# An attention kernel fused with a feed-forward layer: the order of the first steps' state, masks and weight casts, and of the last group's products

## The chip, the cores and the metric

The kernel runs on one core of a Trainium2 chip. The metric is the device time of one launch in microseconds (us); a smaller time is better. The median of three runs before the change is 206.12 us (206.1 to 206.34).

A core has five engines with an instruction queue each: TensorE (PE, matmuls, with PEld for its weight loads), VectorE (DVE), ScalarE (ACT), GpSimd (POOL) and SyncE (SP), which here only issues transfers. The engines run side by side, each in the order of its own queue, and wait for one another through semaphores. Matmul results go to PSUM; all other data of the core is in SBUF.

## The reference

Decayed linear attention in blocks of 64 tokens, then a feed-forward layer on its output. Inputs are float32; `q`, `k`, `v` have 4 batches, 8 heads, 768 tokens and 64 features.

```python
for b in range(nb):
    intra = einsum('bhic,bhjc->bhij', qb, kb) * Dmask      # Dmask = lam ** (i - j), lower triangle
    intra = einsum('bhij,bhjd->bhid', intra, vb)
    inter = einsum('bhid,bhde->bhie', qb * lam_pow, kv_state)
    out[:, :, sl] = intra + inter
    kv_state = lam_block * kv_state + einsum('bhsd,bhse->bhde', kb * rev_pow, vb)
x = attn_out.transpose(0, 2, 1, 3).reshape(3072, 512)
h = x @ w_in                      # 512 x 2048
out = gelu_tanh(h) @ w_out        # 2048 x 512
```

## The kernel before

**Attention steps.** The attention is cut into 24 steps. A step `s` is 256 tokens of one batch (a superblock, `sbg = s // 2`) and four of the eight heads (`half = s % 2`). Inside, the 256 tokens are two chunks `c` of 128. For each step:

- `prep_qk` and `prep_v` scale q and v by the decay and convert q, k and v to 16 bits (DVE, ACT, POOL); `stage_t` transposes q and k on PE into `Tps` and copies them to `qkT` (L245 to L251: which engine copies depends on the step).
- `scores` makes k times q in the PSUM tile `Sps`; `causal` (L280, DVE) multiplies it by the mask into `PT`.
- `products(n, s)` does two things on PE. For step `n` it makes the new part of the state, K, in columns 256 to 383 of the two PSUM tiles `OK` (L306). For step `s` it makes the output in columns 0 to 255: values times `PT` (L320), plus state `u` times q (L329). It takes two new PSUM tiles unless it is given `banks`.
- `update(s, c, parts)` carries the state on: part "t" (L366, DVE) reads K from `OK`, part "u" (L373, POOL) makes the 16-bit `u` that L329 reads.
- `x_out` (L343, ACT) copies the output of a step to `xT`, the transposed input of the feed-forward layer.

**Feed-forward groups.** The tokens are done in seven groups of 256 or 512 (L380). Group 0 is superblocks 0 and 1, thus steps 0 to 3. Its rows of `h` come from `mm1_part` (rows f = 0 to 7) and `mm1` (8 to 15): four matmuls over the 128-row pieces c of `x`, where pieces 0 and 1 are heads of the even steps and 2 and 3 those of the odd steps. A stage of `mm1_part` names the pieces, the token blocks (b0, b1 or both) and if it is the last, after which the GELU follows on ACT. Weights arrive as float32 and are cast: `cast_win` (L105 on ACT, L107 on DVE) for `w_in`, others for `w_out`.

From group 2 on the second product is done with seven half-sized products instead of eight (a Strassen-like scheme): `product(m, p)` for m in 3, 4, 5, 2, 1, 7, 6 and a pair p of 128-row tiles. Products 4 and 3 lie in PSUM tile A, 5 and 2 in B, 1 in C, 7 and 6 in D; for the last pair of all, 6 has a tile E. After product 2, ACT copies B (L477, L478) and DVE makes all four quarters of `o` from A and B (L481, L482); after product 1 DVE adds C to the two diagonal quarters (L490), after 7 and 6 it adds D (L502), in the last pair one quarter each (L497). Then the rows are stored.

**Order.** Everything is recorded in program order per engine (`pin`). Feed-forward work stands as small pieces in the list `filler`, and `fill(n)` puts the next n pieces at that place. The order of the first steps is written out by hand (L600 to L652). The last group's order is the product list built at L546 to L551.

PSUM tiles other than `Sps` share six buffers (`ps_M`), so a new tile waits until an old one is free.

Of the kernel before, what the change touches and what calls it, by code (L numbers as in the profile page):

```python
# [15 lines left out]
def kernel(  # L16
# [217 lines left out]
    def stage_t(s):  # L234
        if s >= FIRST_DMA_T:
            return
        tq, tk = a16[s][:2]
        Tps = ps_M.tile([P, 2, 2, 2, P], FP16, tag="M", name="Tps")
        for i, t in enumerate((tq, tk)):
            for hp in range(2):  # L240
                for j in range(2):
                    pin(nc.tensor.transpose(Tps[:, i, j, hp, :], t[:, j, 2 * hp : 2 * hp + 2, :],  # L242
                                            ident[:]))
        o = qkp.tile([P, 2, 2, 2, P], FP16, tag="qkT", name=f"qkT_{s}")
        if s == 2:  # L245
            pin(nc.scalar.activation(out=o[:, 0], in_=Tps[:, 0], func=AF.Copy))
            pin(nc.vector.tensor_copy(out=o[:, 1], in_=Tps[:, 1]))
        elif s in (1, 3, 5, 6):
            pin(nc.scalar.activation(out=o[:], in_=Tps[:], func=AF.Copy))
        else:  # L250
            pin(nc.vector.tensor_copy(out=o[:], in_=Tps[:]))  # L251
        qkT[s] = o
# [80 lines left out]
            x_out(s, OK)  # L333
        return OK, opened

    def x_out(s, OK):
        sbg, half = divmod(s, 2)
        g, i = group_of[sbg]
        if g not in xT:
            xT[g] = xtp.tile([P, 2, len(groups[g]), 2, SB], FP16, tag="xT", name=f"xT_{g}")  # L340
        dst = xT[g][:, half, i]
        for c in range(2):
            pin(nc.scalar.activation(  # L343
                out=dst[:, :, c * P : (c + 1) * P].rearrange("p hp (t j) -> p hp j t", j=2),
                in_=OK[c][:, 0:256].rearrange("p (hp j t) -> p hp j t", hp=2, j=2),
                func=AF.Copy))

    us = {}

# [34 lines left out]
    def queue_group(g):  # L384
# [60 lines left out]
                i = slice(i0, i1)  # L445
                pin(nc.vector.tensor_tensor(gsum[m][:, i, :], block(T0, F0, i), block(T1, F1, i), op))  # L446

        of_pair = {}
        PLACE = {4: ("A", 0), 3: ("A", 1), 5: ("B", 0), 2: ("B", 1), 1: ("C", 0), 7: ("D", 0),
                 6: ("D", 1)}  # L450

        def product(m, p):

            banks = of_pair.setdefault(p, {})
            name, half = PLACE[m]
            final = g == len(groups) - 1 and p == HN // P - 1
            if final and m == 6:
                name = "E"
            if m in (3, 5, 1, 7) or name == "E":
                banks[name] = ps_M.tile([P, 2, HE], FP32, tag="M", name=f"M{name}")  # L460
            dst = banks[name][:, half]
            t = slice(p * P, p * P + P)
            for i in range(HF):
                lhsT = block(*G_PLAIN[m], i)[:, t] if m in G_PLAIN else gsum[m][:, i, t]
                if m in W_PLAIN:
                    F, E = W_PLAIN[m]
                    rhs = w_out16[:, F * HF + i, E * HE : E * HE + HE]
                else:
                    rhs = w_sum16[:, w_slot[m], i, :]
                pin(nc.tensor.matmul(dst, lhsT, rhs, start=(i == 0), stop=(i == HF - 1),  # L470
                                     skip_group_check=True))
            tt = nc.vector.tensor_tensor
            if m == 2:
                o = banks["o"] = otp.tile([P, 2, 2, HE], FP32, tag="o32", name="o32")
                A, B = banks["A"], banks["B"]
                m525 = mtp.tile([P, 3, HE], FP32, tag="m525", name="m525")
                pin(nc.scalar.activation(out=m525[:, 0:2], in_=B[:], func=AF.Copy))  # L477
                pin(nc.scalar.activation(out=m525[:, 2], in_=B[:, 0], func=AF.Copy))  # L478
                flat = o[:].rearrange("p e t d -> p (e t) d")
                banks["diag"] = flat[:, 0:4:3]  # L480
                pin(tt(banks["diag"], A[:], m525[:, 0:2], ALU.subtract))  # L481
                pin(tt(flat[:, 1:3], A[:], m525[:, 1:3], ALU.add))  # L482
                if final:
                    for T, queue in ((1, nc.sync), (0, nc.scalar)):
                        row = row0 + T * HN + p * P
                        E = slice((1 - T) * HE, (1 - T) * HE + HE)
                        pin(queue.dma_start(out=out[row : row + P, E], in_=o[:, 1 - T, T, :]))
            elif m == 1:
                d = banks["diag"]
                pin(tt(d, banks["C"][:, 0].unsqueeze(1).to_broadcast([P, 2, HE]), d, ALU.add))  # L490
            elif final and m in (7, 6):

                o, T = banks["o"], (0 if m == 7 else 1)
                row = row0 + T * HN + p * P
                rows = out[row : row + P, :].rearrange("q (e d) -> q e d", e=2)
                d = o[:, T, T, :]
                pin(tt(d, banks[name][:, half], d, ALU.add))  # L497
                queue = nc.scalar if m == 7 else nc.sync
                pin(queue.dma_start(out=rows[:, T], in_=d))
            elif m == 6:  # L500
                d = banks["diag"]
                pin(tt(d, banks["D"][:], d, ALU.add))  # L502
                for T in range(2):
                    row = row0 + T * HN + p * P
                    pin(nc.sync.dma_start(out=out[row : row + P, :].rearrange("q (e d) -> q e d", e=2),
                                          in_=banks["o"][:, :, T, :]))
# [2 lines left out]

        def mm1_part(f, cs, blocks, last):  # L510

            if cs[0] == 0:
                first[f] = ps_M.tile([P, N], FP32, tag="M", name="Hps")
            for c in cs:
                pin(nc.tensor.matmul(by_block(first[f][:])[:, blocks],  # L515
                                     w_in16[:, c, f * P : (f + 1) * P], x(c)[:, blocks],
                                     start=(c == 0), stop=last and c == NC - 1,
                                     skip_group_check=True))
            if last:
                pin(nc.scalar.activation(out=gT[:, f % HF, f // HF, :], in_=first.pop(f)[:],  # L520
                                         func=AF.Gelu_apprx_tanh))

        if g == 0:
            both, b0, b1 = slice(0, 2), slice(0, 1), slice(1, 2)
            for fs, stages in ((range(4), (((0, 1), both, False), ((2, 3), b0, False),
                                           ((2, 3), b1, True))),
                               (range(4, 8), (((0, 1), both, False), ((2, 3), both, True)))):
                for stage in stages:
                    for f in fs:
                        filler.append(lambda f=f, stage=stage: mm1_part(f, *stage))  # L530
            for f in range(8, NF):
                filler.append(lambda f=f: mm1([f]))
            order = [(tau, part) for part in (0, 2, 1, 3) for tau in range(3)]
            order += [(3, part) for part in (0, 2, 1, 3)]
            for tau, part in order:
                filler.append(lambda tau=tau, part=part: mm2(tau, part))
            return
# [3 lines left out]
        if g == 1:  # L541
# [1 line left out]
                for part in (0, 2, 1, 3):  # L543
                    filler.append(lambda tau=tau, part=part: mm2(tau, part))
            return
        ms = ((3, 4, 5, 2), (1, 7, 6))  # L546
        order = [(m, p) for p in range(HN // P) for m in ms[0] + ms[1]]
        if g == len(groups) - 1:
            order = [(m, p) for part in ms for p in range(HN // P) for m in part]
        for m, p in order:  # L550
            filler.append(lambda m=m, p=p: product(m, p))  # L551

        def behind(k, i0, i1):

# [24 lines left out]
    def fill(n):  # L579
        for _ in range(min(n, len(filler))):  # L580
            filler.pop(0)()
# [36 lines left out]
    stage_t(2)  # L618
    prep_qk(3)
    update(1, 0)  # L620
    idle(3)
    scores(2)
    products(2, None)
    causal(2)
    prep_v(3)
    update(2, 0)
    update(1, 1)
    update(2, 1, "t")
    idle(2)
    stage_t(3)  # L630
    OK1 = products(None, 1, evacuate=False)[0]
    OK2 = products(None, 2, evacuate=False)[0]
    x_out(2, OK2)
    x_out(1, OK1)
    scores(3)
    banks = products(3, None)
    update(3, 0)
    c01, c23 = slice(0, 2), slice(2, 4)
    cast_win(0, 0, 256, 128, c01)
    cast_win(0, 256, 512, 256, c01, on_act=True)  # L640
    causal(3)
    queue_group(0)
    fill(4)
    products(None, 3, banks)
    cast_win(0, 0, 512, 256, c23)
    fill(8)
    cast_win(1, 0, 512, 256, c01)
    update(3, 1, "t")
    cast_win(1, 0, 512, 256, c23)
    fill(8)  # L650
    update(2, 1, "u")
# [83 lines left out]
```

## Time and profile before

The profiled execution took 206.1 us; its span, from the first to the last instruction, is 204.3 us.

| engine | busy us | share of the span | instructions |
|---|---|---|---|
| PE | 196.8 | 96% | 2321 |
| DVE | 144.8 | 71% | 271 |
| ACT | 107.7 | 53% | 204 |
| POOL | 70.1 | 34% | 80 |

The first 13.4 us hold the warm-up of PE (matmuls on ones), the first loads and steps 0 and 1. Transfers run at 381 GB/s from 13.4 to 20.7 us: inputs and weights come in one after the other on SP's queue. A profile row gives line, engine, operation, output and input tiles, count, then busy time and the mean of one; a timeline row begins with start and duration in us, and ends with the engine's idle time before it and what released it. Busy time of PE is that of pipelined matmuls, whose ends are modelled.

### The profile page before, as it was taken

How to read it: one execution, taken by the hardware profiler on the slowest of the kernel's cores; microseconds unless marked ns; L12 is line 12 of the kernel's file. 1: busy time of each engine (PE TensorE's matmuls, PEld its weight loads, DVE VectorE, ACT ScalarE, POOL GpSimd, SP SyncE). 2: the span in 40 equal slices, each digit the busy share in tenths (PEclk: the TensorE clock that was granted, in tenths of full speed). 3: DMA queues.
4: the chain of work that ended last, by engine and by line, in shares of the span. 5: the costliest groups of instructions: out<-in, count | busy, mean ns of one | idle time of the engine just before them, and what ended most of it. 6: DMA issues, size and time to landing. Idle time of an engine off the chain costs nothing.

```text
span 204.3 us, 5584 instructions
## 1 busy us (share of the span) xinstructions
PE 196.8 (96%) x2321; PEld 127.6 (62%) x2321; DVE 144.8 (71%) x271; ACT 107.7 (53%) x204; POOL 70.1 (34%) x80
## 2 busy tenths in 40 slices
PE   7888999999999999999999999999999999999992
PEld 2454644456875788654688654788554788545881
DVE  4887627867599999929997828996739673136552
ACT  2364678475683573477722477641576331577110
POOL 5595123646487750436134404314412100000000
PEclk9999999999999999999999999999999999999999
DMA  4999999999999999996449993647330003300014
GB/s 132 299 321 385 387 388 379 285 291 315 297 262 228 296 241 173 235 285 176 91 128 266 181 279 94 152 107 156 75 85 0 0 3 103 107 0 0 3 51 156
DMA packets 64074, 37.86 MB, mean 185 GB/s; under 512 B 17712, under 2 KB 59184, under 8 KB 64048
## 3 DMA queue, kind: packets, MB, share of 16 engines
q1 hardware_dynamic: 63760, 37.24, 68.1%
q8 instruction: 18, 0.29, 0.6%
q10 hardware_dynamic: 288, 0.26, 0.4%
q14 instruction: 8, 0.07, 0.1%
HBM read 27.27 MB, written 6.29 MB: 164 GB/s over the span
## 4 chain that ended last, share of the span: by engine, by line
PE 89%; DMA 3%; SPq 2%; ACT 1%; DVE 1%; issue 1%
PE Hps L401 37%; PE O2ps L416 10%; PE MB L470 8%; PE MA L470 7%; PE MD L470 7%; PE Sps L271 4%; PE MC L470 4%; PE Hps L515 4%; PE OK L329 3%; PE OK L320 3%; DMA k<-in_k_dram 3%; SPq L68 2%; PE OK L306 1%; PE Tps L242 1%; DVE t L366 1%
## 5 line engine op out<-in xcount | busy, mean ns | idle before, releaser
L401 PE MATMUL Hps<-xT,w_in 128*128 128x512 f16 (+1 forms) x416 | 79.1, 346 | 0.0
L405 ACT ACTIVATE gT<-Hps 128x512 f16<-128x512 f32 x88 | 52.1, 598 | 21.9 <-PE Hps L401 21.1
L401 PEld LDWEIGHTS <-w_in 128*128 128x128 f16 x416 | 40.2, 98 | 33.5
L373 POOL TENSOR_TENSOR u<-t,lumask 128x256 f16<-128x256 f32 x40 | 31.4, 792 | 80.6 <-DVE t L366 58.4
L446 DVE TENSOR_TENSOR gs<-gT 128x512 f16<-128x512 f16 (+1 forms) x70 | 36.6, 586 | 10.8 <-ACT gT L405 10.6
L280 DVE TENSOR_TENSOR PT<-Sps,mask 128x1024 f16<-128x1024 f32 x24 | 29.2, 1216 | 17.1 <-PE Sps L271 17.1
L470 PEld LDWEIGHTS <-gs 128*128 128x128 f16 x360 | 34.9, 98 | 4.0
L211 POOL TENSOR_TENSOR v<-v,dv 128x512 f16<-128x512 f32 x24 | 29.2, 1220 | 4.9 <-DMA v<-in_v_dram 4.8
L343 ACT ACTIVATE xT<-OK 128x256 f16<-128x256 f32 x48 | 18.2, 454 | 20.0 <-PE OK L329 14.3
L416 PE MATMUL O2ps<-w_out,gT 128*128 128x512 f16 x96 | 21.9, 379 | 0.0
L226 ACT ACTIVATE qk<-k 128x512 f16<-128x512 f32 x24 | 15.0, 626 | 9.3 <-DMA k<-in_k_dram 9.3
L221 DVE TENSOR_TENSOR qk<-q,dq 128x512 f16<-128x512 f32 x23 | 19.3, 841 | 0.0
L477 ACT ACTIVATE m<-MB 128x512 f32<-128x512 f32 x9 | 5.4, 597 | 25.4 <-PE MB L470 25.4
L470 PE MATMUL MA<-w_sum,gT 128*128 128x256 f16 x144 | 17.5, 273 | 0.1
L470 PE MATMUL MD<-w_sum,gs 128*128 128x256 f16 x136 | 17.5, 273 | 0.0
L470 PE MATMUL MB<-w_out,gs 128*128 128x256 f16 x144 | 17.2, 273 | 0.0
L366 DVE SCALAR_TENSOR_TENSOR t<-t,lamu,OK 128x64 f32<-128x64 f32 x64 | 14.5, 273 | 2.3 <-PE OK L306 1.1
L470 PEld LDWEIGHTS <-gT 128*128 128x128 f16 x144 | 14.0, 98 | 2.8 <-ACT gT L405 0.3
L416 PEld LDWEIGHTS <-gT 128*128 128x128 f16 x96 | 9.2, 98 | 9.9
L481 DVE TENSOR_TENSOR o<-MA,m 128x512 f32<-128x512 f32 x9 | 6.2, 688 | 12.3 <-ACT m L477 12.3
L271 PEld LDWEIGHTS <-qkT 64*64 64x64 f16 x384 | 6.2, 106 | 8.6 <-issue 4.2
L123 DVE TENSOR_TENSOR w_sum<-wo,wo 128x1024 f16<-128x1024 f32 x6 | 7.9, 1362 | 4.2 <-DMA wo<-in_moe_w_out_dram 4.2
(55 smaller groups left out, 168.8 us busy)
## 6 DMA issues: line engine op xcount, KB each, us to landing
q<-in_q_dram SPq DMA_DIRECT2D x24, 256.0 KB, 4.5
k<-in_k_dram SPq DMA_DIRECT2D x24, 256.0 KB, 4.9
v<-in_v_dram SPq DMA_DIRECT2D x24, 256.0 KB, 4.9
out_dram<-o SPq DMA_DIRECT2D x22, 256.0 KB, 4.1
wo<-in_moe_w_out_dram SPq DMA_DIRECT2D x4, 1024.0 KB, 9.2
wi<-in_moe_w_in_dram SPq DMA_DIRECT2D x4, 512.0 KB, 8.0
wi<-in_moe_w_in_dram SPq DMA_DIRECT2D x2, 1024.0 KB, 12.5
out_dram<-o SPq DMA_DIRECT2D x2, 128.0 KB, 1.9
```

The costliest lines, as they stand in the source:

```text
L211: pin(nc.gpsimd.tensor_tensor(wide(tv[:]), ld32[s][2][:], decay(dv, s), ALU.mult))
L221: pin(q_eng.tensor_tensor(wide(tq), q32[:], decay(dq, s), ALU.mult))
L226: pin(nc.scalar.activation(out=wide(tk), in_=k32[:], func=AF.Copy))
L280: pin(nc.vector.tensor_tensor(t[:].rearrange("p a b c d -> p (a b) (c d)"), Ss.pop(n)[:].rearrange("p a b c d -> p (a b) (c d)"), mask[:]. ...
L343: pin(nc.scalar.activation(out=dst[:, :, c * P : (c + 1) * P].rearrange("p hp (t j) -> p hp j t", j=2), in_=OK[c][:, 0:256].rearrange("p ( ...
L366: pin(nc.vector.scalar_tensor_tensor(t[:, hp, :], state[half][:, hp, :], lamu[:, 2 * half + hp : 2 * half + hp + 1], K[:, hp, :], ALU.mult ...
L373: pin(nc.gpsimd.tensor_tensor(u[:], state[half][:].unsqueeze(2).to_broadcast([P, 2, 2, D]), lumask[:, 2 * half : 2 * half + 2, :].unsqueez ...
L401: pin(nc.tensor.matmul(by_block(Hps[:, i, :]), w_in16[:, c, f * P : (f + 1) * P], x(c), start=(c == 0), stop=(c == NC - 1)))
L405: pin(nc.scalar.activation(out=dst, in_=Hps[:], func=AF.Gelu_apprx_tanh))
L416: pin(nc.tensor.matmul(O2[tau][0][:], gT[:, f % HF, f // HF, tau * P : (tau + 1) * P], w_out16[:, f, :], start=(n == 0), stop=(n == NF - 1)))
L446: pin(nc.vector.tensor_tensor(gsum[m][:, i, :], block(T0, F0, i), block(T1, F1, i), op))
L470: pin(nc.tensor.matmul(dst, lhsT, rhs, start=(i == 0), stop=(i == HF - 1), skip_group_check=True))
```

## The change

Five edits, in the order of the diff:

- The copy of `qkT` of step 3 is split: half on ACT, half on DVE, as that of step 2 was.
- `x_out` can put the second chunk on another engine. Step 3 uses it, with DVE.
- In the last group the product order is now pair by pair, all seven products of pair 0, then all of pair 1. Before, products 3, 4, 5, 2 of both pairs came first. The two stores of off-diagonal quarters right after product 2 are gone: with product 7 the lower one goes out on SP, and the upper rows in one store of 256 KB on ACT.
- The first rows f = 0 to 3 of group 0 do pieces 0 and 1 by token blocks as well: 16 matmuls of 256 columns instead of 8 of 512.
- The hand-written order of steps 2 and 3: the states of steps 1 and 2 ahead of step 2's mask; step 2's output into the tiles that hold its own K; steps 1 and 2 evacuated in that order; the second state of step 2 after its evacuation; the casts of `w_in` ahead of step 3's state and mask; part of the casts on ACT; step 3's output after ten filler pieces instead of four.

```diff
-        if s == 2:
+        if s in (2, 3):
             pin(nc.scalar.activation(out=o[:, 0], in_=Tps[:, 0], func=AF.Copy))
             pin(nc.vector.tensor_copy(out=o[:, 1], in_=Tps[:, 1]))
-        elif s in (1, 3, 5, 6):
+        elif s in (1, 5, 6):
...
-    def x_out(s, OK):
+    def x_out(s, OK, second=None):
...
         for c in range(2):
-            pin(nc.scalar.activation(
-                out=dst[:, :, c * P : (c + 1) * P].rearrange("p hp (t j) -> p hp j t", j=2),
-                in_=OK[c][:, 0:256].rearrange("p (hp j t) -> p hp j t", hp=2, j=2),
-                func=AF.Copy))
+            d = dst[:, :, c * P : (c + 1) * P].rearrange("p hp (t j) -> p hp j t", j=2)
+            o = OK[c][:, 0:256].rearrange("p (hp j t) -> p hp j t", hp=2, j=2)
+            if c == 1 and second is not None:
+                pin(second.tensor_copy(out=d, in_=o))
+            else:
+                pin(nc.scalar.activation(out=d, in_=o, func=AF.Copy))
...
-                if final:
-                    for T, queue in ((1, nc.sync), (0, nc.scalar)):
-                        row = row0 + T * HN + p * P
-                        E = slice((1 - T) * HE, (1 - T) * HE + HE)
-                        pin(queue.dma_start(out=out[row : row + P, E], in_=o[:, 1 - T, T, :]))
...
+                if m == 7:
+                    low = row0 + HN + p * P
+                    pin(nc.sync.dma_start(out=out[low : low + P, 0:HE], in_=o[:, 0, 1, :]))
                 d = o[:, T, T, :]
                 pin(tt(d, banks[name][:, half], d, ALU.add))
-                queue = nc.scalar if m == 7 else nc.sync
-                pin(queue.dma_start(out=rows[:, T], in_=d))
+                if m == 7:
+                    pin(nc.scalar.dma_start(out=rows, in_=o[:, :, 0, :]))
+                else:
+                    pin(nc.sync.dma_start(out=rows[:, 1], in_=d))
...
-            if cs[0] == 0:
+            opens = f not in first
+            if opens:
...
-                                     start=(c == 0), stop=last and c == NC - 1,
+                                     start=opens and c == 0, stop=last and c == NC - 1,
...
-            for fs, stages in ((range(4), (((0, 1), both, False), ((2, 3), b0, False),
-                                           ((2, 3), b1, True))),
+            for fs, stages in ((range(4), (((0, 1), b0, False), ((0, 1), b1, False),
+                                           ((2, 3), b0, False), ((2, 3), b1, True))),
...
-        ms = ((3, 4, 5, 2), (1, 7, 6))
-        order = [(m, p) for p in range(HN // P) for m in ms[0] + ms[1]]
-        if g == len(groups) - 1:
-            order = [(m, p) for part in ms for p in range(HN // P) for m in part]
-        for m, p in order:
-            filler.append(lambda m=m, p=p: product(m, p))
+        for p in range(HN // P):
+            for m in (3, 4, 5, 2, 1, 7, 6):
+                filler.append(lambda m=m, p=p: product(m, p))
...
     update(1, 0)
+    update(1, 1, "t")
     idle(3)
     scores(2)
-    products(2, None)
+    banks = products(2, None)
+    update(2, 0)
     causal(2)
     prep_v(3)
-    update(2, 0)
-    update(1, 1)
-    update(2, 1, "t")
+    update(1, 1, "u")
     idle(2)
     stage_t(3)
-    OK1 = products(None, 1, evacuate=False)[0]
-    OK2 = products(None, 2, evacuate=False)[0]
-    x_out(2, OK2)
-    x_out(1, OK1)
+    products(None, 1)
+    products(None, 2, banks)
+    update(2, 1, "t")
     scores(3)
     banks = products(3, None)
-    update(3, 0)
     c01, c23 = slice(0, 2), slice(2, 4)
     cast_win(0, 0, 256, 128, c01)
     cast_win(0, 256, 512, 256, c01, on_act=True)
+    update(3, 0)
     causal(3)
     queue_group(0)
-    fill(4)
-    products(None, 3, banks)
-    cast_win(0, 0, 512, 256, c23)
     fill(8)
-    cast_win(1, 0, 512, 256, c01)
+    cast_win(0, 0, 256, 256, c23, on_act=True)
+    cast_win(0, 256, 512, 256, c23)
+    fill(2)
+    products(None, 3, banks, evacuate=False)
+    x_out(3, banks[0], nc.vector)
+    fill(6)
     update(3, 1, "t")
+    cast_win(1, 0, 512, 256, c01)
     cast_win(1, 0, 512, 256, c23)
```

The diff also puts the tiles of a pair into one dictionary for all pairs, since pairs no longer overlap.

More of the change, by code (lines that the diff above doesn't have):

```diff
@@ L446, in sum_g @@
                 pin(nc.vector.tensor_tensor(gsum[m][:, i, :], block(T0, F0, i), block(T1, F1, i), op))
-        of_pair = {}
+        banks = {}
         PLACE = {4: ("A", 0), 3: ("A", 1), 5: ("B", 0), 2: ("B", 1), 1: ("C", 0), 7: ("D", 0),
@@ L452, in product @@
         def product(m, p):
-            banks = of_pair.setdefault(p, {})
             name, half = PLACE[m]
@@ L640 @@
     cast_win(0, 256, 512, 256, c01, on_act=True)
+    update(3, 0)
     causal(3)
     queue_group(0)
-    fill(4)
-    products(None, 3, banks)
-    cast_win(0, 0, 512, 256, c23)
     fill(8)
+    cast_win(0, 0, 256, 256, c23, on_act=True)
[4 more added lines that the diff above has]
+    fill(6)
+    update(3, 1, "t")
     cast_win(1, 0, 512, 256, c01)
-    update(3, 1, "t")
     cast_win(1, 0, 512, 256, c23)
```

## The prediction

> **What bounds the kernel now.** I read the busy time by stage first, then who TensorE (PE) waits for, then the timeline of the two places that the diff touches. The stages, cut where PE becomes gapless and where its last product ends:
>
> ```profile
> core 0: us, PE busy (x) PEld busy (x) DVE busy (x) ACT busy (x) POOL busy (x), PEclk, DMA share, GB/s
> ...
> 13.40:20.70 7.30, 6.27 (x140) 3.74 (x141) 5.88 (x16) 3.49 (x7) 4.69 (x7) 1.00 1.06 381
> 20.70:200.50 179.80, 179.74 (x2056) 118.86 (x2052) 129.16 (x227) 98.59 (x188) 56.79 (x57) 1.00 0.67 174
> 200.50:204.30 3.80, 0.03 (x1) 0.00 (x0) 0.42 (x1) 0.00 (x0) 0.00 (x0) 0.99 0.47 154
> ```
>
> From 20.7 to 200.5 us PE is busy 179.74 of 179.80 us at full clock. Nothing but matmul work counts there, so time can move at two ends only: the head (13.4 to 20.7, 1.03 us of PE idle) and the tail (3.8 us). The waits of PE, with those of the idle warm-up left out:
>
> ```profile
> PE Hps L515 <- DVE w_in L107: 0.8, 1, 0.8
> PE Sps L271 <- DVE qkT L247: 0.5, 1, 0.5
> PE OK L320 <- DVE t L366: 0.2, 1, 0.2
> ```
>
> The L271 wait is before 13.4 and untouched. The other two, 1.0 us together, are what the new order could win. The timeline of the head:
>
> ```profile
> 13.88 1.23 DVE L280 TENSOR_TENSOR PT<-Sps,mask 128x1024 f16<-128x1024 f32 x1 [0.33 <-PE Sps L271]
> 15.02 1.23 DVE L366 SCALAR_TENSOR_TENSOR t<-t,lamu,OK 128x64 f32<-128x64 f32 x6
> 16.59 1.37 ACT L343 ACTIVATE xT<-OK 128x256 f16<-128x256 f32 x4 [0.59 <-PE OK L329]
> 17.74 0.93 DVE L107 CAST w_in<-wi 128x256 f16<-128x256 f32 x2
> 17.90 1.24 POOL L373 TENSOR_TENSOR u<-t,lumask 128x256 f16<-128x256 f32 x2 [0.99 <-DVE t L366]
> ```
>
> The reader sees step 2's mask, six state operations, four evacuations, then the two casts that open the first rows. The second cast runs beside a POOL operation. Last, the tail:
>
> ```profile
> 199.49 1.04 PE L470 MATMUL ME<-w_sum,gs 128*128 128x256 f16 x8
> 199.69 0.42 DVE L497 TENSOR_TENSOR o<-MD,o 128x256 f32<-128x256 f32 x1 [0.18 <-PE MD L470]
> 200.15 0.34 ACTq L499 DMA_DIRECT2D out_dram<-o  x1
> 200.56 0.42 DVE L497 TENSOR_TENSOR o<-ME,o 128x256 f32<-128x256 f32 x1 [0.45 <-PE ME L470]
> 201.01 0.36 SPq L499 DMA_DIRECT2D out_dram<-o  x1
> ```
>
> DVE waits for PE before each of the last two adds: it has caught up. What leaves last is two 128 KB stores. For these two the DMA view gives landings 2.1 us (ACT) and 1.7 us (SP) after issue, so the end is 201.01 + 1.75 = 202.76, and the span closes 1.57 us later.
>
> **What the Trainium skill says.** "SBUF — State Buffer", section "Who interferes with whom": a DVE cast can take the port pair shared with GpSimd, and whoever is second is blocked for the other's whole instruction. The trace agrees: of the two 128x256 casts, shortest 0.285 us and mean 0.504, the slow one (0.72) started at 17.94, inside POOL's 17.90 to 18.52. "PSUM — Partial Sum Buffer", "PSUM bank collisions raise a hardware error": two engines must not touch one bank and quadrant together, even at different columns. So an evacuation by ACT and a state read by DVE from the same bank are serialized; before, step 3's L366 started at 21.65, after ACT's last evacuation at 21.56. "DMA: Bandwidth & Descriptors", "Issuing engines are not separate DMA queues": stores of SP and ACT share the same 16 engines. The trace moves 337 GB/s from 199.9 to 201.8 with both queues loaded.
>
> **Head, step by step.** Durations are those of the rows above and of their groups; a DVE operation follows its predecessor 0.19 us after its start if 64 wide, PE starts 0.05 us after a DVE end, DVE 0.04 after ACT or PE.
>
> Step 2's state ahead of its mask: t of step 1 (second half) at 13.67 and 13.87, t of step 2 at 14.06 and 14.25, so the mask starts at 14.44 instead of 13.88 and ends at 15.66 instead of 15.11. Cost 0.55 us on PT. The split copy of qkT 3 ends at 16.04 (ACT 14.98 to 15.58, then DVE 0.42), before it was 16.00: nothing. Step 2's values times PT may start at 15.71; before, after its first matmul at 15.54, PE stood until 15.92 for the state of step 1, since that bank was being freed. Own banks remove that: 0.21 us won. PE then needs 0.35 + 0.35 us for L320 and L329, reaches the scores of step 3 at 16.41 (before 16.62) and its K product ends at 17.10 (17.31).
>
> New wait: the second state of step 2 reads the bank that now also holds step 2's output, so it waits for ACT's evacuation. That starts 0.32 us after L329's start 16.06, ends at 17.14; state at 17.18 and 17.38. Queued behind it on DVE are the two casts: 17.57 to 17.86 and 17.77 to 18.05, at 0.285 us each because POOL's next operation (u of step 3) now comes after them. Before they ended 18.03 and 18.67. The weights landed at 10.10 + 7.1 = 17.2 us, so they hold no one. PE opens the first rows at 17.91 (18.08) and is not stopped a second time: 16 matmuls of 256 columns, at 0.109 us each (8 take 0.87 in the chain of waits), equal the 8 of 512 at 0.216. The 8 extra instructions cost nothing, since a weight load of 0.098 us fits under 0.109. With two more pieces (4 x 0.109) PE reaches step 3's output at 20.08; ACT's cast for them ends at 19.24 (landed 10.98 + 7.6 = 18.6, plus 0.64), step 3's mask at 19.57, both in time. Add 0.1 for the switch of tile shape, as before: 20.18, and 20.76 at its end. Before, 20.71, with 0.44 us less done: lead 0.38 us.
>
> What is late next: the last pieces of these rows need step 3's evacuation. Before, eight pieces (0.87 us) covered it, ending 21.58 against 21.56. Now four cover it, until 21.20. The DVE half of the evacuation is in no row; I price it as the 128x256 L497, 0.42 us, both read PSUM in f32 (ends: 0.28 as 128x128 L363, 0.69 as the 128x512 ones). It starts when the last L329 ends, 20.53 + 0.40 + 0.04 = 20.97, and PE may go on at 21.44: 0.24 us stand. Lead left: 21.6 - 21.44 = 0.16; I take **0.2 us**. Two bounds: this wait gone and the casts right at the landing (PE at 17.2 + 0.29 + 0.05 = 17.55) give 0.16 + 0.24 + 0.36 = 0.76; the evacuation at 0.69 and one cast locked behind POOL's 0.61 give -0.3. Later stages keep the lead: the w_in casts of parts 2 and 3 end 1.3 us or more before their rows, and step 4's k is cast 0.7 us before its transposes. SP's weight loads are issued up to 0.5 us earlier or 0.3 later, but 381 GB/s in this stage says that the queue, not the issue, sets their landing.
>
> **Tail, step by step.** PE's work is the same; the last three products (C, D, E of the last pair) still end at 200.53. But product 2 of that pair now ends just ahead of them, when C starts at 197.74, instead of four products earlier. ACT's copy starts 0.20 later, 197.94, and takes 0.60; then DVE has L481 at 198.57, L482 at 199.18, L490 at 199.78 (spacing 0.61, 0.60 as in the same sequence at 171.85, 172.46, 173.06), ending 200.46. The add of D follows, 200.55 to 200.97, the add of E at 200.90 to 201.32. DVE, not PE, ends last: 0.34 us later.
>
> The stores: the two early ones of the last pair are gone; a lower quarter goes on SP at 199.9 and is out before the rest. ACT now sends both halves of the upper rows, 256 KB, when D is added: issue 201.0. A 256 KB store with its twin lands in 2.5 to 2.6 us where the queues are otherwise free (168.7 to 175.8); ACT's ran 0.16 slower than SP's at 197.27. So 201.0 + 2.65 = 203.65 at most, plus up to 0.39 (128 KB at 337 GB/s) shared with SP's last store, less up to 0.4 because a single store need not wait for its twin. In its favour, the other pair's 512 KB have left before. I take 203.7, **0.95 us** later than 202.76. Bounds: 0.5 (no gap between dependent adds, no sharing) and 1.2.
>
> **Sum.** 0.95 - 0.2 = 0.75 us slower. The profiled execution took 206.1 us at a span of 204.3; the median of the three runs is 206.12, the same execution in effect. Forecast 206.85 us, span 205.05. The measurement can tell 0.2%, 0.41 us.
>
> **Rivals.** (1) Forecast, lead 0 to 0.45 and tail 0.6 to 1.15: 206.25 to 207.2, chance 0.72. (2) No change: the lead is near 0.7 because step 3's evacuation does not stop PE, and the ACT store lands in 2.2 us as ACT's 128 KB did: 206.1 - 0.7 + 0.5 = 205.9 up to 206.4. For it, the 1.0 us of waits in the head; against it, double the bytes. 0.14. (3) Faster: the ACT store lands before SP's last one, so that only DVE's 0.34 us counts at the end, and the casts run at the weights' landing, lead 0.76: 205.7. It decides once the tail costs less than the lead. Against it, the state of step 2 ahead of the casts on DVE, which cannot start before 17.18. 0.04. (4) Worse: the evacuation takes 0.69, POOL locks a cast under which PE waits, lead -0.3, tail 1.2: 207.6. 0.10.
>
> Of (1) some 0.06 lies within 0.2%. So slower 0.76, same 0.20, faster 0.04. Range 206.3 to 207.3.
>
> **What would show it.** Right: PE's first rows at about 17.9 without a second stop; a PE wait of some 0.2 us for DVE's evacuation near 21.2; L403 starting 0.2 us earlier than L401 did (25.93); the two last adds with no idle time ahead of them; a 256 KB ACT store that lands last or with SP's, 2.4 to 2.9 us after issue. Wrong: PE waiting for the E product before the last add, or a landing under 2.2 us (tail too dear); first rows before 17.7 and no wait near 21.2 (lead too small).

## The result and the profile after

The changed kernel takes 207.74 us (median of four runs, 207.47 to 208.02); the kernel before took 206.11 us beside it (205.95 to 206.34). The ratio is 1.0078, with a 95% interval of 1.0059 to 1.0097. The forecast was 206.85 us, at most 207.3: the direction was right, the loss is twice the one predicted. The profiled execution of the changed kernel took 207.53 us at a span of 205.8.

The stages of the changed kernel, in the view of busy time by stretches (columns: stretch and its length, busy us and count for each engine, clock, share of the DMA engines' time, GB/s):

```profile
core 0: us, PE busy (x) PEld busy (x) DVE busy (x) ACT busy (x) POOL busy (x), PEclk, DMA share, GB/s
13.40:20.70 7.30, 5.89 (x144) 4.52 (x148) 5.71 (x16) 3.74 (x8) 4.91 (x8) 1.00 1.06 382
20.70:200.70 180.00, 179.84 (x2068) 118.61 (x2060) 129.13 (x227) 98.77 (x187) 56.87 (x57) 1.00 0.68 174
200.70:205.80 5.10, 0.01 (x1) 0.00 (x0) 0.76 (x2) 0.00 (x0) 0.00 (x0) 0.87 0.31 104
```

The middle is nearly as full of PE work as it was: 0.16 us of idle PE in 180.00, before 0.06 in 179.80. The stretch behind the last product, 3.8 us before, is now 5.1. From the first second-product matmul (O2ps) to the start of the last product (E) it is 166.65 us before and 166.63 after: between head and tail nothing changed.

The waits of PE, those of the warm-up left out:

```profile
PE Hps L517 <- DVE w_in L107: 0.9, 1, 0.9
PE Sps L271 <- DVE qkT L247: 0.5, 1, 0.5
PE OK L320 <- DVE PT L280: 0.2, 1, 0.2
```

The wait for the first weight cast (0.8 before) is not shorter. The wait of L320 was for a state operation that freed a bank; now it is for step 2's mask, the operation that has moved back. The head in the timeline:

```profile
14.71 1.22 DVE L280 TENSOR_TENSOR PT<-Sps,mask 128x1024 f16<-128x1024 f32 x1
15.78 1.63 ACT L348 ACTIVATE xT<-OK 128x256 f16<-128x256 f32 x4
17.50 0.47 DVE L368 SCALAR_TENSOR_TENSOR t<-t,lamu,OK 128x64 f32<-128x64 f32 x2 [1.16 <-ACT xT L348]
17.89 0.49 DVE L107 CAST w_in<-wi 128x256 f16<-128x256 f32 x2
18.23 2.36 PE L517 MATMUL Hps<-xT,w_in 128*128 128x256 f16 x20 [0.93 <-DVE w_in L107]
21.30 0.45 DVE L346 CAST xT<-OK 128x256 f16<-128x256 f32 x1 [0.99 <-PE OK L329]
21.80 2.28 PEld L517 LDWEIGHTS <-w_in 128*128 128x128 f16 x16 [0.38 <-DVE xT L346]
```

In this execution step 2's scores begin at 13.72 us instead of 13.41, ahead of everything the diff touches. That start lies between 13.41 and 14.09 in the twelve profiles of this study, whichever head they have. Read the rows 0.31 us earlier to compare them with the prediction. The reader sees DVE stand 1.16 us for ACT's evacuation, with the two casts queued behind it, and further down the weight loader stand 0.38 us for DVE's half of step 3's evacuation.

The tail in the timeline, and the landings of the stores in the view of transfers (operation, KB each, median us from issue to landing):

```profile
199.68 1.04 PE L471 MATMUL ME<-w_sum,gs 128*128 128x256 f16 x8
200.75 0.42 DVE L496 TENSOR_TENSOR o<-MD,o 128x256 f32<-128x256 f32 x1
201.09 0.41 DVE L496 TENSOR_TENSOR o<-ME,o 128x256 f32<-128x256 f32 x1
201.21 0.65 ACTq L498 DMA_DIRECT2D out_dram<-o  x1
201.53 0.36 SPq L500 DMA_DIRECT2D out_dram<-o  x1
```

```profile
out_dram<-o SPq DMA_DIRECT2D x2, 128.0 KB, 2.2
out_dram<-o ACTq DMA_DIRECT2D x1, 256.0 KB, 2.8
```

The two adds stand without idle time ahead of them, as predicted: DVE, not PE, is last. The trace gives the single landings: ACT's 256 KB 2.82 us after issue, SP's last 128 KB 2.67 us after, where the same store took 1.74 before. From the start of E to the last landing it is 4.52 us, before 3.27. The stretches behind it show how those stores went:

```profile
201.60:202.40 0.80, 0.00 (x0) 0.00 (x0) 0.00 (x0) 0.00 (x0) 0.00 (x0) 1.00 0.00 0
202.40:203.80 1.40, 0.00 (x0) 0.00 (x0) 0.00 (x0) 0.00 (x0) 0.00 (x0) 1.00 0.83 281
```

For 0.8 us no data moves at all, with every earlier store gone; then 384 KB leave in one stream. The trace also records each DMA packet with its queue, start and size. By these records the stream runs from 202.51 to 203.79 us, 307 GB/s, and the last landing follows 0.41 us later. ACT's packets open it; the first of SP's comes at 203.06, 1.52 us after its issue, where a 128 KB store of SP's needs 0.87 us in this same run with the queues empty (issue at 200.08, first packet at 200.95).

So the 1.42 us that the span grew in this pair of profiles are 0.31 (late start), -0.12 (head, from the start of step 2's scores to E), 1.25 (tail) and -0.02 (from the last landing to the end).

### The profile page after: what moved, and what is told of

The parts are those of the page before. It is cut to its first block, busy times and chain, and to the rows that moved or that the text cites. A ratio compares the mean times of both kernels' runs of the same rounds, so it can differ in the third digit from the quotient of the medians.

```text
span 205.8 us, 5599 instructions
## 1 busy us (share of the span) xinstructions
PE 196.8 (96%) x2329; PEld 128.4 (62%) x2329; DVE 144.8 (70%) x272; ACT 108.1 (53%) x204; POOL 70.1 (34%) x80
## 4 chain that ended last, share of the span: by engine, by line
PE 88%; DMA 3%; SPq 2%; DVE 2%; ACT 2%; issue 1%; DVEq 0%
PE Hps L403 37%; PE O2ps L418 10%; PE MB L471 8%; PE MA L471 7%; PE MD L471 7%; PE MC L471 4%; PE Sps L271 3%; PE Hps L517 3%; PE OK L329 3%; DMA k<-in_k_dram 3%; PE OK L320 3%; SPq L68 2%; PE Tps L242 1%; PE OK L306 1%; ACT xT L348 1%; DVE t L368 1%
## 5 line engine op out<-in xcount | busy, mean ns | idle before, releaser
L221 DVE TENSOR_TENSOR qk<-q,dq 128x512 f16<-128x512 f32 x23 | 19.2, 835 | 0.0
```

The source lines that it names most:

```text
L221: pin(q_eng.tensor_tensor(wide(tq), q32[:], decay(dq, s), ALU.mult))
```

## The experiments

Each was timed in five rounds beside the kernel before, which had a median of 206.33 to 206.36 us in these longer series (25 to 57 runs). The ratios given are the record's; they differ a little from those of the medians. "E to landing" is the time from the start of the last product, E, to the last landing in that run's profile: 3.27 us before, 4.52 after.

**Which part costs: head or tail alone.** e1_tail has the head of before and the whole tail of the change (order and stores); e2_head the reverse.

```diff
-        ms = ((3, 4, 5, 2), (1, 7, 6))
-        order = [(m, p) for p in range(HN // P) for m in ms[0] + ms[1]]
-        if g == len(groups) - 1:
-            order = [(m, p) for part in ms for p in range(HN // P) for m in part]
+        for p in range(HN // P):
+            for m in (3, 4, 5, 2, 1, 7, 6):
...
+                if m == 7:
+                    pin(nc.scalar.dma_start(out=rows, in_=o[:, :, 0, :]))
```

The diff shows the core of what e1_tail takes over; e2_head takes over every other hunk and none of these.

> The last group's new order and its new stores alone, with the head of the kernel before. Theory A (the whole loss sits in the tail: from the start of the last product to the last landing 4.52 us against 3.27): 1.25 us slower, 207.3 to 207.5, the last product starting where it did before. Theory B (the head costs time too): 0.9 us slower or less.

> The new order of the first steps alone, with the tail of the kernel before. Theory A (the head gives back 0.1 us on PE, and the 0.31 us by which the profile of the changed kernel started late belongs to that run): 0.1 us faster, 205.9 to 206.1. Theory B (the late start comes with the new program): 0.2 us slower or more, 206.3 to 206.6, and the scores of step 2 start near 13.7 again.

e1_tail took 207.58 us (207.34 to 209.05, 10 runs), ratio 1.0069 [1.0044, 1.0093]; e2_head 206.21 us (22 runs), ratio 0.9999 [0.9987, 1.0011], between its two theories. The tail is the whole loss that can be told from zero. Its E to landing is 4.52 us, as in the full change. The head shows no gain in time. In its profile the stall that the prediction named stands again (timeline):

```profile
21.62 0.45 DVE L346 CAST xT<-OK 128x256 f16<-128x256 f32 x1 [1.00 <-PE OK L329]
22.12 0.44 PEld L518 LDWEIGHTS <-w_in 128*128 128x128 f16 x5 [0.38 <-DVE xT L346]
```

**Order or stores.** e3_order_only takes the pair-by-pair order but keeps the four 128 KB stores of before; e4_stores_only keeps the order of before and takes the new stores. The diff is that of e3_order_only against e1_tail; for e4_stores_only the product list of before was put back into e1_tail.

```diff
+                if final:
+                    for T, queue in ((1, nc.sync), (0, nc.scalar)):
...
+                        pin(queue.dma_start(out=out[row : row + P, E], in_=o[:, 1 - T, T, :]))
...
-                if m == 7:
-                    low = row0 + HN + p * P
-                    pin(nc.sync.dma_start(out=out[low : low + P, 0:HE], in_=o[:, 0, 1, :]))
...
-                if m == 7:
-                    pin(nc.scalar.dma_start(out=rows, in_=o[:, :, 0, :]))
-                else:
-                    pin(nc.sync.dma_start(out=rows[:, 1], in_=d))
+                queue = nc.scalar if m == 7 else nc.sync
+                pin(queue.dma_start(out=rows[:, T], in_=d))
```

> Kernel before, with the last group's products pair by pair, but with the early quarter stores and the 128 KB stores of before. Theory C (the large store is what costs): only the lag of DVE, 0.35 to 0.5 us slower, last landing 1.75 to 1.9 us after its issue. Theory D (the order costs, since the stores of the last pair fall together whatever their size): 0.8 us slower or more.

> Kernel before, with the product order of before, but the stores of the changed kernel (lower quarter with product 7, 256 KB on ACT, 128 KB on SP). Theory C: 0.5 to 0.9 us slower, since the 128 KB store on SP is held up behind the 256 KB one on ACT. Theory D: 0.3 us slower or less, since DVE is not late.

e3_order_only took 206.72 us, ratio 1.0022 [1.0008, 1.0035]; E to landing 3.63 us. Its last stores (timeline, then the stretch in which they move):

```profile
200.61 0.42 DVE L497 TENSOR_TENSOR o<-MD,o 128x256 f32<-128x256 f32 x1
200.95 0.41 DVE L497 TENSOR_TENSOR o<-ME,o 128x256 f32<-128x256 f32 x1
201.07 0.34 ACTq L499 DMA_DIRECT2D out_dram<-o  x1
201.39 0.36 SPq L499 DMA_DIRECT2D out_dram<-o  x1
```

```profile
201.90:202.80 0.90, 0.00 (x0) 0.00 (x0) 0.00 (x0) 0.00 (x0) 0.00 (x0) 1.00 0.88 291
```

The order alone costs 0.36 us of E to landing, as theory C said: DVE's last add starts 0.34 us later after E's start, and both stores land 1.77 and 1.78 us after issue. e4_stores_only took 206.51 us, ratio 1.0009 [0.9992, 1.0025]: not told from no change, so theory C missed its time. Its E to landing is 3.93 us, 0.66 more than before, but its span closes 1.12 us after that instead of 1.57. The missing 0.45 us lies among SP's last instructions, behind every landing; why is open. The two parts do not add: 0.36 and 0.66 of landing make 1.02, together they make 1.25.

**Is it SP's queue, or the size of the store.** In e8_swapped the two last stores change queues. In e5_two_stores ACT sends the upper rows as two stores of 128 KB, the right one first.

Against e1_tail, first e8_swapped, then e5_two_stores:

```diff
-                    pin(nc.scalar.dma_start(out=rows, in_=o[:, :, 0, :]))
+                    pin(nc.sync.dma_start(out=rows, in_=o[:, :, 0, :]))
...
-                    pin(nc.sync.dma_start(out=rows[:, 1], in_=d))
+                    pin(nc.scalar.dma_start(out=rows[:, 1], in_=d))
```

```diff
-                    pin(nc.scalar.dma_start(out=rows, in_=o[:, :, 0, :]))
+                    for e in (1, 0):
+                        pin(nc.scalar.dma_start(out=rows[:, e], in_=o[:, e, 0, :]))
```

> The tail of the changed kernel on the head of the kernel before, with the queues of the last two stores swapped: 256 KB on SP, the last 128 KB on ACT. Theory E: the same time as the tail alone within 0.2 us, the last store again 2.6 us or more from issue to landing. Rival (it is SP's queue that is slow to start a store here): the last store lands within 2.1 us, 0.7 us slower.

> The tail of the changed kernel on the head of the kernel before, but with the 256 KB store on ACT cut into two of 128 KB from the same place. Theory E (the bytes that leave after the last adds set the end): as the tail alone, 1.2 to 1.4 us slower, last landing 4.5 us after the start of the last product. Theory F (one long store holds up the store of the other queue behind it): SP's last store lands within 2.1 us of its issue, 0.7 to 0.9 us slower in all.

e8_swapped took 207.26 us (207.19 to 208.89, 6 runs), ratio 1.0048 [1.0034, 1.0061]. Its profile fell on the 208.89 us run, in which step 2's scores and the second products are 21.09 us apart (19.3 to 19.7 in the other runs with the head of before); only its tail is read here (timeline):

```profile
202.69 0.55 SPq L496 DMA_DIRECT2D out_dram<-o  x1
203.03 0.37 ACTq L498 DMA_DIRECT2D out_dram<-o  x1
```

SP's 256 KB take 2.71 us to land, ACT's 128 KB behind them 2.54: the store behind is held up on either queue, and a slow SP queue is ruled out as the cause. The first packet of ACT's store comes 1.45 us after its issue, against 1.52 for SP's in the changed kernel. Theory E is not met to the letter: the time is 0.32 us below that of e1_tail, the landing a little under 2.6. SP takes 0.10 us less than ACT to issue its 256 KB (0.55 against 0.65), and E to landing is 0.12 us shorter (4.40); the rest of the 0.32 is not explained. e5_two_stores took 206.52 us, ratio 1.0016 [1.0005, 1.0027], less than either theory said; E to landing 3.63. But this was no clean test: the right quarter waits only for an early add, so ACT sent it at 200.39, and two stores of 128 KB were left for the end, as in e3_order_only. Size of the store and bytes left for the end changed at once. The clean version followed.

**Three stores of 128 KB, all late.** e9_two_late is e5_two_stores with the left quarter first; the right one is queued behind it on ACT, so the same 384 KB leave at the end as in e1_tail.

```diff
-                    for e in (1, 0):
+                    for e in (0, 1):
```

> The head of before, the order and the quarters of the changed kernel's tail, but its 256 KB store of the upper rows is cut into two of 128 KB, both on ACT and both behind the add of D (left quarter first), so the same 384 KB leave in the same last 0.7 us as in e1_tail. Theory A (it is the volume that leaves at the end which holds up the last store): SP's 128 KB still take about 2.6 to 2.7 us from issue, ACT's second about as long, time 207.4 to 207.8 us. Theory B (one long store holds up what is issued behind it; three of 128 KB would not): SP's 128 KB take 1.75 to 2.0 us, ACT's second store, issued near ME start + 1.9, lands at + 3.7 to 3.9, time 206.7 to 207.0 us.

It took 207.16 us (207.14 to 207.36, 5 runs), ratio 1.0047 [1.0035, 1.006]; E to landing 4.06 us: between the two theories. Timeline and stretches:

```profile
201.49 0.86 ACTq L497 DMA_DIRECT2D out_dram<-o  x2
201.82 0.36 SPq L499 DMA_DIRECT2D out_dram<-o  x1
```

```profile
201.80:202.30 0.50, 0.00 (x0) 0.00 (x0) 0.00 (x0) 0.00 (x0) 0.00 (x0) 1.00 0.00 0
202.30:203.60 1.30, 0.00 (x0) 0.00 (x0) 0.00 (x0) 0.00 (x0) 0.00 (x0) 1.00 0.92 302
```

SP's store is no longer held up (1.84 us), and ACT's second one, issued last, lands last (2.12). Both theories were half of it, as the packet records of these tails show (the first packet of each stream is ACT's):

| kernel | ACT issue, us | issue takes | first packet after issue | KB in the stream | stream lasts | last landing after it | E to landing |
|---|---|---|---|---|---|---|---|
| e3_order_only | 201.07 | 0.34 | 0.84 | 256 | 0.91 | 0.35 | 3.63 |
| e9_two_late | 201.49 | 0.38 | 0.88 | 384 | 1.29 | 0.36 | 4.06 |
| e1_tail | 201.55 | 0.65 | 1.30 | 384 | 1.28 | 0.40 | 4.52 |
| after | 201.21 | 0.65 | 1.30 | 384 | 1.28 | 0.41 | 4.52 |

From e3_order_only to e9_two_late the stream is 128 KB longer (0.38 us; 0.43 in all). From e9_two_late to e1_tail the bytes are the same, but the issue of 256 KB takes 0.27 us longer and the first packet comes 0.42 us later (0.46 in all). So the 1.25 us of the whole tail have three parts: 0.36 for the order, 0.43 for the 128 KB more that are left for the end, 0.46 for sending 256 KB as one store. The medians say the same: 206.35, 206.72, 207.16 and 207.58 us are 0.37, 0.44 and 0.42 apart. In every row E to landing is 1.53 us from E's start to ACT's issue plus the columns of the first packet, the stream and the last landing, to within 0.01 us.

**Where the head's gain went.** e6_cover is e2_head with step 3's output two filler pieces earlier, so that eight pieces stand behind DVE's half of the evacuation. e7_cast_first also puts the casts ahead of step 2's second state, out of the wait for ACT, with nine pieces ahead and seven behind.

First e6_cover against e2_head, then e7_cast_first against e6_cover:

```diff
-    fill(2)
     products(None, 3, banks, evacuate=False)
     x_out(3, banks[0], nc.vector)
-    fill(6)
+    fill(8)
```

```diff
-    update(2, 1, "t")
     scores(3)
     banks = products(3, None)
     cast_win(0, 0, 256, 128, c01)
     cast_win(0, 256, 512, 256, c01, on_act=True)
+    update(2, 1, "t")
...
+    fill(1)
     products(None, 3, banks, evacuate=False)
     x_out(3, banks[0], nc.vector)
-    fill(8)
+    fill(7)
```

> New head on the tail of before, with step 3's output after eight pieces and eight pieces behind it as cover of its evacuation, instead of ten and six. If the stop of PE at the DVE half of the evacuation is real and costs 0.25 us, it goes: no gap of PE near 21.7, 0.2 to 0.3 us faster than the new head alone, 205.9 to 206.1 where that takes 206.2. If PT of step 3 takes its place, PE waits at L320 and nothing is won.

> As the kernel with the better cover (nine pieces ahead, seven behind), and the second state of step 2 behind the casts of w_in on DVE instead of ahead of them. If the new wait of that state for ACT's evacuation holds up the casts, they start at the weights' landing, first rows at 17.5 to 17.6 us, 0.4 to 0.6 us faster than before: 205.7 to 205.9. If the casts then run into another wait (the weights land later than 17.2), as the kernel with the better cover.

e6_cover took 206.1 us, ratio 0.9985 [0.9974, 0.9997]; e7_cast_first 206.04 us, ratio 0.9984 [0.9975, 0.9993]. Both are faster than the kernel before, by some 0.3 us; against e2_head the medians gain 0.11 and 0.17 us, and the intervals overlap. From step 2's scores to the first second-product matmul e6_cover takes 19.05 us against 19.33 of e2_head: the 0.28 us are the stall for DVE's evacuation, which is gone (timeline):

```profile
20.54 1.90 PEld L518 LDWEIGHTS <-w_in 128*128 128x128 f16 x18
20.60 2.13 PE L518 MATMUL Hps<-xT,w_in 128*128 128x256 f16 x17
20.80 0.45 DVE L346 CAST xT<-OK 128x256 f16<-128x256 f32 x1 [0.56 <-PE OK L329]
```

In e7_cast_first the casts run as soon as the weights have landed. The last two rows are those of step 4:

```profile
17.34 0.50 DVE L107 CAST w_in<-wi 128x256 f16<-128x256 f32 x2 [0.69 <-DMA wi<-in_moe_w_in_dram]
17.69 0.33 PEld L518 LDWEIGHTS <-w_in 128*128 128x128 f16 x4 [0.29 <-DVE w_in L107]
21.16 1.42 PEld L518 LDWEIGHTS <-w_in 128*128 128x128 f16 x12 [0.16 <-DVE xT L346]
38.76 1.52 DVE L221 TENSOR_TENSOR qk<-q,dq 128x512 f16<-128x512 f32 x1
40.34 0.45 PEld L242 LDWEIGHTS <-qk 128*128 128x128 f16 x8 [0.49 <-DVE qk L221]
```

PE opens the first rows at 17.69 us, in e6_cover at 18.16. The landing of the weights sets this start, and not step 2's scores: those began at 14.03 us here and at 13.69 in e10_split_last below, which has the same head and opens the rows at 17.60. Seven pieces cover the evacuation less well than eight (0.16 us stand again). About half of the lead over e6_cover is lost again at step 4: its first transposes (L242) cannot start before DVE has scaled and converted q (L221), which ends at 40.28. e7_cast_first reaches the second products 0.29 us ahead of e6_cover and these transposes 0.14 us ahead (40.34 against 40.48); from the second products to E it takes 166.80 instead of 166.63 us. In e10_split_last the weight loads of these transposes wait 0.60 us, and the stretch is 166.91. So in time e7_cast_first missed its 205.7 to 205.9 us and is not told from e6_cover.

**Splitting the last store.** e10_split_last is e7_cast_first with the last 128 KB cut by rows, one half on SP, one on ACT.

```diff
-                queue = nc.scalar if m == 7 else nc.sync
-                pin(queue.dma_start(out=rows[:, T], in_=d))
+                if m == 7:
+                    pin(nc.scalar.dma_start(out=rows[:, T], in_=d))
+                else:
+                    for queue, q in ((nc.sync, slice(0, 64)), (nc.scalar, slice(64, P))):
+                        pin(queue.dma_start(out=rows[q, T], in_=d[q]))
```

> The kernel e7_cast_first (206.04 us), with the last store of all (the lower right quarter, 128 KB on SP) cut by rows into two of 64 KB, one on SP and one on ACT, both behind the add of E. If the landing depends on the bytes of the last store: 1.75 us from issue falls to 1.3 to 1.5 and the time to 205.6 to 205.8 us. If it is mostly a fixed delay, or if ACT's second issue (queued behind its 128 KB one) comes late: 1.7 to 1.8, time 206.0 to 206.1 us.

It took 206.52 us, ratio 1.0011 [1.0004, 1.0017]. A miss on both sides: it is slower. Both issues start together and take longer than that of the whole store (0.36):

```profile
200.67 0.52 SPq L504 DMA_DIRECT2D out_dram<-o  x1
200.68 0.54 ACTq L504 DMA_DIRECT2D out_dram<-o  x1
```

The halves land 1.98 and 2.24 us after issue instead of 1.74; E to landing is 3.77 us against 3.28 in e7_cast_first.

## Why the prediction was right and wrong

**Where the loss is.** Right: the tail, none in the middle, little in the head. The sum was 0.95 - 0.2 = 0.75 us. In the profiles the terms are 1.25 and 0.12; in time the tail alone costs 1.23 us (e1_tail, 207.58 - 206.35) and the head wins nothing. 1.25 - 0 on the 206.35 us of the long series gives 207.6. So of the 0.89 us between forecast and result, 0.30 are the tail, 0.20 the head and some 0.25 the base: the forecast stood on one execution of 206.1 us, whose step 2 began earliest of all twelve profiles. The remaining 0.1 to 0.2 us of the four runs after are of the size by which starts differ from run to run, and are not traced further.

**The adds.** Right. Predicted from DVE's spacing: add of D at 200.55, of E at 200.90, E starting at 199.49. Measured: 1.07 and 1.41 us after E's start, predicted 1.06 and 1.41. e3_order_only shows that this is worth 0.36 us by itself.

**The landing: the step that failed.** The prediction let ACT issue at 201.0 (201.02, once the 0.19 us by which E starts later is taken off), landed its 256 KB at most 2.65 us later, added up to 0.39 us for SP's store in the same stream, and then took off up to 0.4 us "because a single store need not wait for its twin". The last landing was put at 203.7; on the same clock it came at 204.20 - 0.19 = 204.01. The sum without the deduction is 204.04. The deduction was the mistake: it had no row behind it. That the rest comes so near is partly luck: ACT's store landed 2.82 us after its issue and SP's 0.17 us behind it, where the sum had 2.65 and 0.39. The runs show that the store without a twin does not land early: its first packet leaves only after its own long issue (1.30 us from the start of the issue instead of 0.84), and from there on every byte of both queues counts, at 303 to 307 GB/s in the streams of 384 KB. The other pair's 512 KB "have left before" was set down as a point in its favour; in fact the engines stood idle for at least 0.8 us because nothing had been issued, though the right quarter of the upper rows was ready (e5_two_stores sends it before the add of D), and all 384 KB came after the add of D. "DMA: Bandwidth & Descriptors", section "Issuing engines are not separate DMA queues", of the Trainium skill says that SP's and ACT's transfers interleave on the same 16 engines, which the packet records bear out (in the changed kernel ACT's packets leave from 202.51 to 203.66 us and SP's from 203.06 to 203.79), and that issuing from several engines saves only the issue time, "usually small relative to the DMA itself"; here a longer issue (0.65 against 0.38 us) came with a first packet 0.42 us later, and the end moved by as much.

**Step 2's state, its own banks, the mask.** Right in each time that the profile shows: with the late start of 0.31 us taken off, step 2's second values times PT start at 15.67 (predicted 15.71), its second state at 17.19 (17.18), the first rows at 17.92 (17.91), DVE's half evacuation at 20.99 (20.97), and PE goes on at 21.49 (21.44). That half evacuation was priced at 0.42 us and took 0.45.

**The lead of 0.2 us.** Wrong in what it was measured against. The single timeline of before had 19.43 us from step 2's scores to the second products. The five other profiles with that head, e8_swapped left out, have 19.27, 19.27, 19.27, 19.37 and 19.69; the new head has 19.33 twice. So the new head's gain of 0.1 us against that one execution lies inside the scatter of the old head. That scatter lies in one place, step 3's scores and K products on PE. First before, then e5_two_stores, one of the three at 19.27 (timeline):

```profile
16.62 0.57 PE L271 MATMUL Sps<-qkT 64*64 64x128 f16 x16
16.95 0.36 PE L306 MATMUL OK<-v,qk 64*64 64x64 f16 x16
```

```profile
17.28 0.42 PE L271 MATMUL Sps<-qkT 64*64 64x128 f16 x16
17.52 0.29 PE L306 MATMUL OK<-v,qk 64*64 64x64 f16 x16
```

From the first start to the last end this is 0.69 us in before and 0.53 in e5_two_stores, and the 0.16 us are the whole difference between 19.43 and 19.27. Why PE is slower here in some executions is open. In the new head the same stretch takes 0.65 us in one profile and 0.54 in the other and the 19.33 stay, as the wait for ACT's evacuation ends later. What the order won it gave back in the two waits that the prediction named, the casts queued behind the wait for ACT and the stall behind step 3's evacuation; e6_cover takes the second away, e7_cast_first the first and part of the second, and both come out 0.15% faster. The prediction also said that later stages keep the lead; for a lead as large as that of e7_cast_first they do not, as step 4's q shows. It had looked at k.

**Rivals.** "No change" needed ACT's store to land in 2.2 us, like one of 128 KB; it took 2.82. "Faster" needed it to land before SP's last one. It did, by 0.17 us, and the tail still cost 1.25, since SP's store was held up behind it. "Worse" (207.6) named the right time for partly wrong reasons: it had the tail at 1.2 us, but the evacuation at 0.69 and a lock of POOL in the head, neither of which came.

## What to carry to other kernels

In tails like these, where the queues have run empty, the end is the issue of the first late store, plus the time to its first packet, plus all bytes that are left by then over the rate of the common stream, plus a landing time: add the terms up over all queues, and take nothing off that no row shows. Send each piece of an output when it is ready; here, joining a ready piece to a late one held the ready one back and lengthened the issue. Smaller is not always better: 128 KB stores beat one of 256 KB, but halves of 64 KB lost. A gain of 0.1 or 0.2 us at a place whose start scatters by more from run to run needs more than one profile to be called a gain.

## What was not expected of the hardware

- At the end of these kernels the issue of a store takes longer with its size, 0.34 to 0.39 us for 128 KB and 0.53 to 0.65 us for 256 KB, save for two stores of 128 KB right behind others of the same queue (0.45 in e9_two_late, 0.61 in e4_stores_only). With nothing else being sent, the first packet follows the end of the issue by another 0.50 us (128 KB) or 0.65 us (256 KB).
- A 128 KB store issued 0.32 to 0.34 us behind one of 256 KB on the other queue sent its first packet 1.45 to 1.53 us after its issue (after, e1_tail, e8_swapped); behind one of 128 KB it was 0.89 and 0.92 us (e3_order_only, e9_two_late).
- Two stores of 64 KB with 64 rows each, issued at once from SP and ACT, took 0.52 and 0.54 us to issue, more than one of 128 KB with 128 rows (0.36), while two of 128 KB issued at once took 0.37 and 0.39. Their stream carried 128 KB in 0.73 us, 180 GB/s; a 128 KB store with 128 rows, alone in the changed kernel, took 0.52 us (250 GB/s). The shared moment is not the cause of that: SP's half had the engines to itself for its first 0.28 us and sent 54 KB, where stores with 128 rows send 87 to 89 KB in as long. Rows and size of the store were not separated.
- From the last landing to the end of the span there are 1.54 to 1.58 us in all runs but e4_stores_only, where it was 1.12.
